# The last inverse-transform stage's table built by masked sines ahead of the work, its factor moved to a neighbouring table, and another order

## The chip, the core and the metric

The kernel runs on one core of a Trainium2 chip. Its time is device time in microseconds (us) of one execution, as a median of several. Engines are named as in the profile: PE (TensorE matmul), PEld (its weight load), DVE (VectorE), ACT (ScalarE), POOL (GpSimd), SP (SyncE, which here only issues DMAs).

## The reference

Two independent sequence mixers over 2048 tokens and 640 channels each; their outputs are set side by side. A is a diagonal complex state space, B is a gated long convolution done by FFT of length 4096.

```python
# A: x [2048, 640]
Lam_bar = exp(dt * Lam);  B_bar = ((Lam_bar - 1) / Lam)[:, None] * Bmat
for t in range(L):
    h = Lam_bar * h + x[t] @ B_bar.T
    hs.append(h)
y_a = 2 * real(hs @ Cmat.T) + x * Dskip
# B: q, k, v [2048, 640]
k_shift = 4-tap causal convolution of k with shift_k
kv  = k_shift * v
y   = irfft(rfft(pad(kv)) * rfft(pad(ssm_k)))[:2048]
y_b = q * (y + kv * ssm_D)
out = concatenate([y_a, y_b], axis=-1)          # bf16
```

## The kernel before

**Part A** works on ten column pairs of states. `up2`, `up1`, `up0a/b/c` (L560 for the input products, L581 for the recurrence steps) build block sums of growing length, `coarse` (`cs_...`, L652 to L666) runs the scan over the 128 blocks, `dn3` to `dn0` (L683, L685) carry the states back down, and `C0` to `C15` (L720) project to the output. `gC` (L550) scales the output matrix. Where the add after a `dn` (`ad...`) is on DVE (L703), DVE adds; where it is on ACT (L701), PE adds instead by one more matmul with the identity (L683) and ACT copies.

**Part B** loads k and v (L775, transposing DMAs), convolves and multiplies them (`cm` L198/L199, `ca` L801, `cx` L802), writes the product to DRAM by rows (`pl`, L808, five planes of 128 channels), reads it back in another layout (`rl`, the relay, L818), and transforms it in two halves of 320 channels. A transform is `s1` (L837 wide form with 16 matmuls, L842 narrow form with 32 smaller ones), evicted by L847; `s2` (L861), evicted by L874; a complex product with the filter's transform (`pp pq py pz`, L885 to L892); then back by `r2` (L906), evicted by L911, and `r1` (L927), whose eviction on DVE (L939) multiplies by q. `h` is the filter (`s1h`, `s2h`), `k` the data; `s1k0_5` is group 5 of half 0. Each of the two filter halves must get `addD` (L770, POOL) before its `s1h`.

The stages' sine tables are made on the chip: an iota and an integer multiply on POOL, then a sine on ACT. They are `F1` (for `s1`), `W` (for `s2`; `w_m` L289, `w_q` L291, `w_s` L296), `IDF` (for `r2`; `i_s` L307) and `G` (for `r1`). `G` is needed last. For it, `tables_G` makes four chunks: `g_m` (L327) and `g_q` (L330) on POOL, `g_s` (L332) on ACT into a scratch piece of buffer `AS`, and then twice `g_k` (L198 on DVE or L199 on ACT), which multiply the chunk by `mk[:, el]`, a column per `el` that is 1/2048 on half of the partitions and 0 on the others. `AS` holds the first transform of half 0 until its product is done, so `tables_G` stands behind `middle(0)`.

All buffers are pieces of one SBUF arena, and dependencies are found from the addresses. The order is not a planner's at run time: the string `ORDER` lists every operation with its engine (T is PE, t is PE with the narrow `s1`, V DVE, A ACT, G POOL, S SP) and its first PSUM bank of eight. Each engine runs its operations in that order. An operation that waits holds up all behind it on its engine. PE's matmuls need a free bank, so a late eviction stops PE.

Of the kernel before, what the change touches and what calls it, by code (L numbers as in the profile page):

```python
# [10 lines left out]
FN = mybir.ActivationFunctionType  # L11
# [7 lines left out]
SC = float(TWO_PI / 2 ** 32 * EPS1)  # L19
# [200 lines left out]
def setup(c):  # L220
# [12 lines left out]
          ins=[I3[:, 0:128]])  # L233
# [26 lines left out]
    P.add("mk2", {V: .12}, lambda e: e.tensor_scalar_mul(out=mk, in0=me, scalar1=1.0 / 2048), outs=[mk], ins=[me])  # L260
# [46 lines left out]
    P.add("i_s", {A: .38}, lambda e: e.activation(out=IDF, in_=qi, func=FN.Sin, bias=npi, scale=SC13), outs=[IDF], ins=[qi, npi])  # L307
    c.p31i, c.mk = p31i, mk


def tables_G(c):
# [10 lines left out]
    for ch in range(4):  # L322
        sn = v("AS", 1024 * ch, 1024)
        ri, bh = ch // 2, ch % 2
        full = v("G", 2048 * ch, 2048)
        qc = full.bitcast(i32)
        P.add("g_m", {G: 1.1}, lambda e, qc=qc, ri=ri, bh=bh: e.iota(  # L327
            qc.rearrange("p (b a) -> p b a", a=32), pattern=[[1, 32], [64, 32]], base=2048 + 2048 * ri + 32 * bh,
            channel_multiplier=0), outs=[full])
        P.add("g_q", {G: 1.9}, lambda e, qc=qc: e.tensor_tensor(out=qc, in0=qc, in1=bc(f41s, [128, 1024]), op=ALU.mult),  # L330
              outs=[full], ins=[full, f41s])
        P.add("g_s", {A: 1.07}, lambda e, qc=qc, sn=sn: e.activation(out=sn, in_=qc, func=FN.Sin, scale=SC), outs=[sn], ins=[full])  # L332
        for el in range(2):
            go = Gt[:, ri, 32 * bh:32 * bh + 32, el, :]
            P.add("g_k", {V: .47, G: 2.9, A: 1.02}, lambda e, go=go, el=el, sn=sn: c.SM[e](go, sn.rearrange("p (b a) -> p b a", a=32), mk[:, el:el + 1]),
                outs=[go], ins=[sn, mk])
# [621 lines left out]
def build(c):  # L958
# [5 lines left out]
    setup(c)  # L964
    params(c)
# [59 lines left out]
    tables_G(c)  # L1025
# [17 lines left out]
def plain_order(P):  # L1043
# [127 lines left out]
```

## Time and profile before

| | us |
|---|---|
| median of 3 runs | 199.77 (199.49 to 200.62) |
| the profiled execution, its own time | 200.44 |
| its span, first to last instruction | 198.7 |
| granted PE clock | 0.999 |

The profile is of one execution. A row of a windows view has a stretch of time, and then how long each engine was busy in it (with its count of instructions); a row of a timeline has start, duration, engine, line and shapes, and in brackets how long the engine had been idle and who ended that; a row of a by-form group has the count, busy us and mean ns of one, and idle time before.

### The profile page before, as it was taken

How to read it: one execution, taken by the hardware profiler on the slowest of the kernel's cores; microseconds unless marked ns; L12 is line 12 of the kernel's file. 1: busy time of each engine (PE TensorE's matmuls, PEld its weight loads, DVE VectorE, ACT ScalarE, POOL GpSimd, SP SyncE). 2: the span in 40 equal slices, each digit the busy share in tenths (PEclk: the TensorE clock that was granted, in tenths of full speed). 3: DMA queues.
4: the chain of work that ended last, by engine and by line, in shares of the span. 5: the costliest groups of instructions: out<-in, count | busy, mean ns of one | idle time of the engine just before them, and what ended most of it. 6: DMA issues, size and time to landing. Idle time of an engine off the chain costs nothing.

```text
span 198.7 us, 7834 instructions
## 1 busy us (share of the span) xinstructions
PE 182.5 (92%) x3493; PEld 121.0 (61%) x3493; DVE 162.3 (82%) x231; ACT 135.1 (68%) x165; POOL 69.1 (35%) x62
## 2 busy tenths in 40 slices
PE   7689999989999997896999799999999999999992
PEld 3344555556565764464566666566777777977761
DVE  3640379779998789999999999899999999958551
ACT  2434499878762859998999798999999940650000
POOL 6759930590000000083200762974600016541200
PEclk9999999999999999999999999999999999999999
DMA  4999999899999999699971796221899524555864
GB/s 93 192 188 155 153 189 133 157 171 188 239 204 225 211 209 120 94 184 148 140 209 49 179 153 136 79 61 38 159 182 178 151 69 132 139 132 125 215 156 142
DMA packets 107739, 30.17 MB, mean 152 GB/s; under 512 B 102586, under 2 KB 107066, under 8 KB 107706
## 3 DMA queue, kind: packets, MB, share of 16 engines
q1 hardware_dynamic: 107418, 29.35, 80.6%
q8 instruction: 27, 0.44, 1.0%
q10 hardware_dynamic: 288, 0.33, 0.6%
q14 instruction: 6, 0.05, 0.1%
HBM read 10.99 MB, written 7.86 MB: 95 GB/s over the span
## 4 chain that ended last, share of the span: by engine, by line
PE 59%; ACT 16%; DVE 9%; SPq 7%; issue 5%; DMA 3%; DVEq 0%; ACTq 0%
PE acc L560 18%; PE acc L720 18%; ACT arena L874 8%; PE acc L906 5%; PE acc L581 4%; SPq L494 3%; PE acc L861 3%; PE acc L927 3%; DMA arena<-in_A_x_dram 3%; SPq L526 3%; DVE arena L847 2%; ACT arena L701 2%; PE acc L685 2%; PE acc L837 2%; ACT arena L554 2%
## 5 line engine op out<-in xcount | busy, mean ns | idle before, releaser
L560 PE MATMUL acc<-arena 128*64 128x512 bf16 x400 | 47.8, 389 | 3.0 <-DMA arena<-in_A_x_dram 2.0
L720 PE MATMUL acc<-arena 128*128 128x320 bf16 x320 | 45.9, 300 | 0.5 <-ACT arena L874 0.4
L560 PEld LDWEIGHTS <-arena 128*64 128x64 bf16 x400 | 24.3, 108 | 22.7 <-issue 4.3
L720 PEld LDWEIGHTS <-arena 128*128 128x128 bf16 x320 | 30.2, 98 | 12.7 <-ACT arena L874 0.6
L874 ACT CAST arena<-acc 128x960 bf16<-128x960 f32 (+1 forms) x40 | 34.9, 916 | 1.3 <-PE acc L861 0.9
L847 ACT CAST arena<-acc 128x1024 bf16<-128x1024 f32 x30 | 29.3, 1028 | 2.9 <-PE acc L842 1.5
L861 PE MATMUL acc<-arena 128*64 128x160 bf16 x512 | 22.9, 235 | 2.0 <-ACT arena L847 0.7
L911 ACT CAST arena<-acc 128x1024 bf16<-128x1024 f32 x16 | 15.9, 1037 | 10.5 <-PE acc L906 10.4
L861 PEld LDWEIGHTS <-arena 128*64 128x64 bf16 x512 | 17.9, 110 | 8.1 <-ACT arena L874 3.0
L722 DVE TENSOR_TENSOR arena<-acc,arena 128x640 bf16<-128x640 f32 x16 | 13.1, 820 | 7.4 <-PE acc L720 7.3
L801 POOL TENSOR_TENSOR arena<-arena 128x2048 bf16<-128x2048 bf16 x1 | 4.1, 4067 | 40.2 <-DVE arena L198 40.2
L712 POOL TENSOR_TENSOR arena<-arena 128x640 bf16<-128x640 bf16 x9 | 12.5, 1398 | 14.8 <-DVE arena L722 8.0
L801 DVE TENSOR_TENSOR arena<-arena 128x2048 bf16<-128x2048 bf16 x14 | 17.1, 1221 | 0.3
L890 POOL TENSOR_TENSOR arena<-arena 128x1280 bf16<-128x1280 bf16 x2 | 5.3, 2668 | 32.8 <-DVE arena L888 20.8
L198 DVE TENSOR_SCALAR arena<-arena 128x2048 bf16<-128x2048 bf16 (+2 forms) x24 | 15.5, 656 | 1.0 <-DMA arena<-in_B_k_dram 0.7
L577 DVE CAST arena<-acc 128x1024 bf16<-128x1024 f32 x5 | 6.0, 1222 | 10.9 <-PE acc L560 10.4
L847 DVE CAST arena<-acc 128x1024 bf16<-128x1024 f32 x10 | 12.0, 1220 | 2.4 <-PE acc L842 1.9
L685 PE MATMUL acc<-arena 128*128 128x512 bf16 (+2 forms) x50 | 13.2, 327 | 0.2 <-ACT arena L874 0.2
L939 DVE TENSOR_TENSOR arena<-acc,arena 128x960 bf16<-128x960 f32 (+1 forms) x12 | 12.2, 1037 | 1.4 <-PE acc L927 1.4
L888 POOL TENSOR_TENSOR arena<-arena 128x1280 bf16<-128x1280 bf16 x4 | 10.6, 2641 | 5.8 <-DVE arena L885 5.8
L885 DVE TENSOR_TENSOR arena<-arena 128x2560 bf16<-128x2560 bf16 x8 | 12.1, 1508 | 0.1
L906 PE MATMUL acc<-arena 64*128 64x128 bf16 x320 | 11.9, 225 | 0.1
(144 smaller groups left out, 294.0 us busy)
## 6 DMA issues: line engine op xcount, KB each, us to landing
out_dram<-arena SPq DMA_DIRECT2D x32, 160.0 KB, 2.7
arena<-in_B_ssm_k_dram SPq DMA_DIRECT2D x8, 320.0 KB, 5.2
kv_rows<-arena SPq DMA_DIRECT2D x5, 512.0 KB, 5.2
arena<-kv_rows SPq DMA_DIRECT2D x16, 160.0 KB, 4.8
arena<-in_A_x_dram SPq DMA_DIRECT2D x16, 160.0 KB, 3.0
arena<-in_B_q_dram SPq DMA_DIRECT2D x8, 320.0 KB, 7.5
arena<-in_A_B_im_dram ACTq DMA_DIRECT2D x1, 160.0 KB, 2.4
arena<-in_A_B_re_dram ACTq DMA_DIRECT2D x1, 160.0 KB, 2.6
```

The lines of the kernel that those rows point to most:

```text
L198: vm = lambda e: lambda out, in_, by: e.tensor_scalar_mul(out=out, in0=in_, scalar1=by)
L560: e.matmul(o[64 * r:64 * r + 64], lhsT=self.BT[j][:, r, d, :], rhs=self.XP[:, d, 2 * q:2 * q + 2], start=(d == 0), stop=(d == 4), skip_gro ...
L685: e.matmul(B[:, o:o + 128 * k], lhsT=c.RR[:, n, j, :], rhs=A[:, j, q:q + k, 0:128], start=not by_pe, stop=True, skip_group_check=True)
L712: P.add(f"xd{i}", {PDVE: dve(640, .52), PPOOL: 1.5}, lambda e: e.tensor_tensor(out=ys, in0=ys, in1=c.DR, op=ALU.mult), outs=[ys], ins=[ys, ...
L720: e.matmul(B[:, 512 * b:512 * b + 320], lhsT=lh[j], rhs=self.CT[:, j, 320 * b:320 * b + 320], start=(j == 0), stop=(j == 9))
L722: P.add(f"ev_C{i}", {PDVE: dve(640)}, lambda e, B: e.tensor_tensor(out=ys.rearrange("p (b n) -> p b n", b=2), in0=B.rearrange("p (b n) -> ...
L801: P.add(f"ca{d}_{j}", tt, lambda e: e.tensor_tensor(out=t1, in0=t1, in1=t2, op=ALU.add), outs=[t1], ins=[t1, t2])
L847: P.add(f"e1{what}{hf}_{u}", {PACT: act(1024), PDVE: dve(1024)}, lambda e, B: c.CP[e](out=out, in_=(B.rearrange("p (l n s k) -> p k s l n" ...
L861: e.matmul(B[64 * s:64 * s + 64, 512 * b + 160 * i:512 * b + 160 * i + 160], lhsT=c.W[:, k, 64 * b:64 * b + 64], rhs=self.AS[hf][:, k, 160 ...
L874: c.CP[e](out=out, in_=b.rearrange("p r (k j n) -> p r k j n", k=n, j=4) if nj > 1 else b.rearrange("p r (k x) -> p r k x", k=n))
L906: e.matmul(B[:, 512 * s + 128 * i:512 * s + 128 * i + 128], lhsT=lh[i][s][r], rhs=rh, start=(r == 0), stop=(r == 1), tile_position=(64 * s ...
L911: P.add(f"er2{hf}_{u}", {PACT: act(1024), PDVE: dve(1024)}, lambda e, B: c.CP[e](out=out, in_=B.rearrange("p (s n b) -> p b s n", s=2, n=4 ...
```

## The change

`tables_G` moves ahead of `params`, so it is the first thing after `setup`. The four `g_s` into scratch and the eight `g_k` go; in their place ACT makes eight sines, two for each chunk, that write `G` directly. The mask is in the sine's scale: `mk` is now `SC` (the factor from integer to angle) on half of the partitions and 0 on the others, one column for each `el`, so the sine's angle is 0 where the table must be 0. The integers of a chunk lie where the next chunk's table will be, those of the last chunk in `Y`. The factor 1/2048 goes into `IDF` by one small multiply on DVE (`i_k`). Every operation gets a new number, and `ORDER` is another list.

```diff
-    P.add("mk2", {V: .12}, lambda e: e.tensor_scalar_mul(out=mk, in0=me, scalar1=1.0 / 2048), outs=[mk], ins=[me])
+    P.add("mk2", {V: .12}, lambda e: e.tensor_scalar_mul(out=mk, in0=me, scalar1=SC), outs=[mk], ins=[me])
...
     P.add("i_s", {A: .38}, lambda e: e.activation(out=IDF, in_=qi, func=FN.Sin, bias=npi, scale=SC13), outs=[IDF], ins=[qi, npi])
+    P.add("i_k", {V: .2}, lambda e: e.tensor_scalar_mul(out=IDF, in0=IDF, scalar1=1.0 / 2048), outs=[IDF], ins=[IDF])
...
     for ch in range(4):
-        sn = v("AS", 1024 * ch, 1024)
         ri, bh = ch // 2, ch % 2
-        full = v("G", 2048 * ch, 2048)
+        full = v("G", 2048 * (ch + 1), 2048) if ch < 3 else v("Y", 0, 2048)
         qc = full.bitcast(i32)
...
-        P.add("g_s", {A: 1.07}, lambda e, qc=qc, sn=sn: e.activation(out=sn, in_=qc, func=FN.Sin, scale=SC), outs=[sn], ins=[full])
         for el in range(2):
             go = Gt[:, ri, 32 * bh:32 * bh + 32, el, :]
-            P.add("g_k", {V: .47, G: 2.9, A: 1.02}, lambda e, go=go, el=el, sn=sn: c.SM[e](go, sn.rearrange("p (b a) -> p b a", a=32), mk[:, el:el + 1]),
-                outs=[go], ins=[sn, mk])
+            P.add("g_s", {A: 1.07}, lambda e, qc=qc, go=go, el=el: e.activation(
+                out=go, in_=qc.rearrange("p (b a) -> p b a", a=32), func=FN.Sin, scale=mk[:, el:el + 1]), outs=[go], ins=[full, mk])
...
     setup(c)
+    tables_G(c)
     params(c)
...
     middle(0)
-    tables_G(c)
     b.load_q(0)
...
-    "122G0 128A0 127A0 8G0 56V0 121S0 0G0 50G0 6T7 82G0 21V0 79G0 116G0 7G0 9V0 41G0 479G0 13G0 93V0 16V0 15V0 19V0 35V0 52V0 14V0 "
+    "140S0 141G0 147A0 75V0 76S0 77S0 8G0 146A0 7G0 9V0 13G0 59G0 0V0 3T1 5T4 21V0 110V0 14V0 18V0 57V0 4T4 15V0 16V0 100G0 19V0 "
```

Lines of the new kernel are one lower from L346 on (L332 is now L334, L847 now L846).

**On ACT**, the stretch of the sines. Before, the four sines (L332) and four of the eight masking multiplies (L199, shape 128x32x32; the other four are on DVE) stand late, among the evictions of the second half's transform and of `r2` (L874, L847, L911). The first piece begins at the first sine:

```order
L332 ACTIVATE arena<-arena 128x1024
L874 CAST arena<-acc 128x2x3x4x40
L332 ACTIVATE arena<-arena 128x1024
L701 CAST arena<-acc 128x8x128
L874 CAST arena<-acc 128x2x3x4x40 x2
L847 CAST arena<-acc 128x64x2x8 x5
L701 CAST arena<-acc 128x8x128
L847 CAST arena<-acc 128x64x2x8 x2
L332 ACTIVATE arena<-arena 128x1024
```

Now (the second piece, from the first eviction of an `up2`, L576) two masked sines (L334) stand near the start, with `sin` of part A (L453), three small exponentials (L368), the first `w_s` (L296), and two multiplies of the convolution (L199) behind them:

```order
L576 CAST arena<-acc 128x2x4x128
L334 ACT_TABLE_LOAD
L334 ACTIVATE arena<-arena 128x32x32 x2
L453 ACTIVATE arena<-arena 128x1280
L368 ACT_TABLE_LOAD
L368 ACTIVATE arena<-arena 128x10 x3
L296 ACT_TABLE_LOAD
L296 ACTIVATE arena<-arena 128x1024
L199 ACTIVATE arena<-arena 128x2048 x2
L394 ACTIVATE arena<-arena 128x80
L576 CAST arena<-acc 128x2x4x128
```

All eight sines and `cos` (L454) now stand ahead of the first eviction of `s2h0`; the table loads are four in all, six before.

**On POOL**, from `addD` of half 0 (L770, now L769) on. Before, one `rr` table (L437), one `g_q` and two `g_m` followed it, then a part of the convolution (L801):

```order
L770 TENSOR_TENSOR arena<-arena 128x80
L437 TENSOR_TENSOR arena<-arena 128x1280
L330 TENSOR_TENSOR arena<-arena 128x1024
L327 IOTA arena 128x1024 x2
L801 TENSOR_TENSOR arena<-arena 128x2048
```

Now three `g_q` (L330) with a `g_m`, then `phc` (L452, which `cos` reads), `r16` (L641, on DVE before) and `gm` (L436, on DVE before) follow it, ahead of the same part of the convolution:

```order
L769 TENSOR_TENSOR arena<-arena 128x80
L330 TENSOR_TENSOR arena<-arena 128x1024
L327 IOTA arena 128x1024
L330 TENSOR_TENSOR arena<-arena 128x1024
L452 TENSOR_TENSOR arena<-arena 128x1280
L641 COPY arena<-arena 128x1280
L330 TENSOR_TENSOR arena<-arena 128x1024
L436 TENSOR_TENSOR arena<-arena 128x1280
L800 TENSOR_TENSOR arena<-arena 128x2048
```

**On SP**, the first loads. Before, behind the first pair of x, both pairs of part A's B matrix (L494) came ahead of the second pair of x (L526) and of the first k (L775):

```order
L526 DMA_TRANSPOSE arena<-in_A_x_dram 128x5x256 x2
L494 DMA_TRANSPOSE arena<-in_A_B_re_dram 128x5x256
L494 DMA_TRANSPOSE arena<-in_A_B_im_dram 128x5x256 x2
L494 DMA_TRANSPOSE arena<-in_A_B_re_dram 128x5x256
L526 DMA_TRANSPOSE arena<-in_A_x_dram 128x5x256 x2
L775 DMA_TRANSPOSE arena<-in_B_k_dram 128x2048
L768 DMA arena<-in_B_ssm_k_dram 32x80x64
L526 DMA_TRANSPOSE arena<-in_A_x_dram 128x5x256 x2
```

Now the second pair of x and the first k stand between the two pairs of B:

```order
L525 DMA_TRANSPOSE arena<-in_A_x_dram 128x5x256 x2
L493 DMA_TRANSPOSE arena<-in_A_B_im_dram 128x5x256
L493 DMA_TRANSPOSE arena<-in_A_B_re_dram 128x5x256
L525 DMA_TRANSPOSE arena<-in_A_x_dram 128x5x256 x2
L774 DMA_TRANSPOSE arena<-in_B_k_dram 128x2048
L493 DMA_TRANSPOSE arena<-in_A_B_im_dram 128x5x256
L493 DMA_TRANSPOSE arena<-in_A_B_re_dram 128x5x256
L525 DMA_TRANSPOSE arena<-in_A_x_dram 128x5x256
```

PE follows: it takes the `up2` of three column pairs with the first B, then the same three with the second pair of x, then those of the second B. Elsewhere the order also moves adds from ACT to DVE (on ACT 11 of 21 before, 6 now), takes the narrow form for 15 of the 40 `s1` groups (25 before), puts three of the sixteen `C` ahead of the second half's `s2k` (four before) and eight between there and the first `r2` of the second half (six before).

72 rows, old and new, of the table ORDER are left out of this document.

## The prediction

> **What bounds the kernel now.** I read the page's busy times first, then a windows view cut where PE starts a new kind of work, then the timeline rows at those cuts, then PE's waits.
>
> ```profile
> PE 182.5 (92%) x3493; PEld 121.0 (61%) x3493; DVE 162.3 (82%) x231; ACT 135.1 (68%) x165; POOL 69.1 (35%) x62
> ```
> ```profile
> core 0: us, PE busy (x) PEld busy (x) DVE busy (x) ACT busy (x) POOL busy (x), PEclk, DMA share, GB/s
> ...
> 20.20:82.70 62.50, 59.47 (x978) 36.44 (x978) 52.50 (x72) 46.56 (x66) 14.13 (x12) 1.00 1.07 180
> 82.70:138.20 55.50, 50.85 (x1210) 33.73 (x1210) 52.92 (x59) 52.38 (x58) 24.70 (x11) 1.00 0.65 121
> 138.20:169.50 31.30, 31.17 (x621) 23.36 (x620) 30.39 (x36) 22.93 (x26) 8.93 (x6) 1.00 0.76 144
> 169.50:195.10 25.60, 25.46 (x588) 19.59 (x584) 17.42 (x19) 5.89 (x6) 6.04 (x5) 1.00 0.66 161
> ```
> ```profile
> 82.73 0.44 PE L842 MATMUL acc<-arena 64*64 64x64 bf16 x32 [0.52 <-ACT arena L874]
> 138.21 1.02 PE L861 MATMUL acc<-arena 128*64 128x160 bf16 x23
> 169.47 1.71 PE L906 MATMUL acc<-arena 64*128 64x128 bf16 x48
> ```
>
> PE's 92% hides stages with different limits. The cuts are the first `s1k0` (82.7), the first `s2k1` (138.2) and the first `r2` of half 1 (169.5). Up to 82.7 PE has gaps. In the **middle** (82.7 to 138.2) PE is busy 50.85 of 55.5, but DVE 52.92 and ACT 52.38: both evicting engines are at 95%, so work on them, not on PE, sets the length. From 138.2 on PE has no gap of note (31.17 of 31.30, 25.46 of 25.60), so PE's work sets it; PE ends at 195.1, and the last stores take 198.7 - 195.1 = 3.6. The start waits for loads:
>
> ```profile
> PE acc L560 <- DMA arena<-in_A_x_dram: 2.0, 2, 1.2
> ```
> ```profile
> 12.36 7.04 PE L560 MATMUL acc<-arena 128*64 128x512 bf16 x60 [0.89 <-DMA arena<-in_A_B_im_dram]
> 20.20 13.82 PE L560 MATMUL acc<-arena 128*64 128x512 bf16 x120 [0.80 <-DMA arena<-in_A_x_dram]
> 14.84 5.23 DMA arena<-in_A_x_dram
> 7.77 3.36 SPq L494 DMA_TRANSPOSE arena<-in_A_B_im_dram  x2
> ```
>
> PE's second group of `up2` waited 0.89 for the first B, the third 0.80 for the second pair of x, whose second transfer (from the chain of waits) started at 14.84 and took 5.23. The last row is SP's: two transposing loads of B hold its queue for 3.36.
>
> This execution took 200.44 us (span 198.7 and 1.74 around it), 0.67 above the median of 199.77. I sum against 200.44 and take 0.67 off at the end. About 0.5%, 1.0 us, is what a measurement of this kernel can tell from no change.
>
> **The tables themselves.**
>
> ```profile
> L332 ACT ACTIVATE arena<-arena 128x1024 bf16<-128x1024 int32 x4 | 4.4, 1112 | 0.0
> L199 ACT ACTIVATE arena<-arena 128x1024 bf16<-128x1024 bf16 x4 | 4.5, 1172 | 0.0
> L198 DVE TENSOR_SCALAR arena<-arena 128x1024 bf16<-128x1024 bf16 x4 | 1.8, 480 | 0.0
> L369 ACT ACT_TABLE_LOAD x2 | 2.6, 1283 | 0.0
> ```
>
> ACT loses 4 x 1.112 + 4 x 1.172 = 9.1 us and gets eight masked sines. No row has one; the nearest is L199, which has the same scale per partition and strided output: 8 x 1.172 = 9.4 (by L332 8.9). DVE loses 4 x 0.480 = 1.9 and gets `i_k`, smaller than L198's rows, at most 0.5. Two of six table loads go, 2 x 1.283 = 2.6. So the totals hardly change; what changes is where the work stands.
>
> ```profile
> 13.18 0.46 ACT L307 ACTIVATE arena<-arena 128x192 bf16<-128x192 int32 x1 [4.68 <-DVE arena L306]
> 13.65 1.28 ACT L369 ACT_TABLE_LOAD   x1
> ```
>
> In these rows a load starts at 13.65, right where the activation before it ends (13.64). [...]
>
> **Up to the first `s1k0`** (82.7 before). Between the same places on PE, sums of rows' means by the two orders give ACT 50.1 to 62.9, less the two loads, so +10.2; DVE 57.0 to 58.9; POOL 22.1 to 33.8; PE 66.7 to 67.9. ACT was busy 46.56 of 62.5 there, so 10 us more fit only if they lie in its gaps. What PE needs at the end of this stretch is the relay:
>
> ```profile
> 68.36 0.57 SPq L808 DMA_DIRECT2D kv_rows<-arena  x1
> 75.69 3.78 SPq L818 DMA_DIRECT2D arena<-kv_rows  x3
> ```
> ```profile
> arena<-kv_rows SPq DMA_DIRECT2D x16, 160.0 KB, 4.8
> ```
>
> The third plane is written at 68.36, after its `cx2` on DVE; the last three reads of half 0 are issued from 75.69, one about 1.26 apart, the last at 78.2, and land 4.8 later, at 83.0: where PE starts (82.73, though by the row its last wait was for an eviction). Now `k2` is loaded ahead of a `C0`, `pl2` has one `C0` less ahead, but four reads come after it besides one `C`, and `coarse` operations stand in DVE's queue before `cx2`. Their sizes are alike, so I leave the relay where it is. For a gain: the second pair of x has two loads of B fewer ahead, so its second transfer starts at 14.84 - 3.36 = 11.5 and lands 5.23 later, at 16.7. PE then has three `up2` with the first B, 2.35 each (7.04 / 3), the second from 12.36, and so wants that x at 12.36 + 2 x 2.35 = 17.1: just in time. That frees the 0.80 before 20.20, and with the other gaps of this stage (62.50 - 59.47 = 3.0) perhaps 2 in all. For a loss: behind its first eviction of an `up2`, near 12.5, ACT has three table loads (3.8), two sines (2.3), `sin`, `w_s`, two multiplies of the convolution and small ones, some 13 in all by their rows. So the next eviction starts near 26, and PE, at 2.35 for each `up2`, needs that bank near 28. If the margin goes, PE waits one to one, some 3 at most. I take **82.9**, bounds 80.7 to 85.7.
>
> **The middle** (55.5 before).
>
> ```profile
> L701 ACT CAST arena<-acc 128x1024 bf16<-128x1024 f32 x9 | 9.2, 1038 | 0.9 <-PE acc L685 0.8
> L703 DVE TENSOR_TENSOR arena<-acc,arena 128x1024 bf16<-128x1024 f32 x8 | 9.7, 1221 | 1.3 <-PE acc L685 1.2
> L847 ACT CAST arena<-acc 128x1024 bf16<-128x1024 f32 x30 | 29.3, 1028 | 2.9 <-PE acc L842 1.5 <-PE acc L837 1.1
> L847 DVE CAST arena<-acc 128x1024 bf16<-128x1024 f32 x10 | 12.0, 1220 | 2.4 <-PE acc L842 1.9 <-PE acc L837 0.5
> L888 DVE TENSOR_TENSOR arena<-arena 128x1280 bf16<-128x1280 bf16 x12 | 9.7, 820 | 0.2
> L801 DVE TENSOR_TENSOR arena<-arena 128x2048 bf16<-128x2048 bf16 x14 | 17.1, 1221 | 0.3
> ```
>
> Between the first `s1k0` and the first `s2k1` ACT loses eight copies of `ad` (8 x 1.038 = 8.3) and three sines (3 x 1.112 = 3.3), and gets two evictions of `s1` (2.1) and two smaller copies (1.4): with small items 57.8 to 49.5. DVE gets four adds (4 x 1.221 = 4.9) and `coarse` work (3.3), and loses two evictions (2.4), one `ca` (1.2), two smaller adds (1.6), five product operations that POOL takes (5 x 0.820 = 4.1), three masking multiplies (1.4), and three evictions of C and gC (2.5): with small items 56.8 to 51.2. PE loses a C (2.8) and most identity matmuls, 46.0 to 39.2, so PE is further from binding.
>
> Before, of 56.8 and 57.8 of work by place 52.92 and 52.38 lay in the time window (0.931, 0.907; the rest ran on either side). The same shares now give 47.7 on DVE and 44.9 on ACT, 92.6 together against 105.3. With the same share of busy time, 55.5 x 92.6 / 105.3 = 48.8; I take **49.0**. Lower bound: DVE without a gap, 47.7. Upper bound: DVE with before's own ratio, 47.7 x 55.5 / 52.92 = 50.0. POOL gets 5 product operations more for this; it was busy 24.70 of 55.5, so it has room.
>
> **From the first `s2k1`** (31.3 and 25.6 before).
>
> ```profile
> L720 PE MATMUL acc<-arena 128*128 128x320 bf16 x320 | 45.9, 300 | 0.5 <-ACT arena L874 0.4
> ```
>
> The cover in PE moved: this stretch gets two C (2 x 45.9 / 16 = 5.7) and four downs that stood in the middle, PE 29.2 to 37.0; DVE 32.4 to 38.5; ACT 25.3 to 21.3. So most of what the middle gains comes back here: PE at 37.0 with 2% of gaps is 37.7, with before's own ratio 37.0 x 31.3 / 29.2 = 39.7. I take **38.4**. DVE, 38.5 x 30.39 / 32.4 = 36.1, stays below. After the first `r2` of half 1 one C goes, PE 25.1 to 22.3: 25.6 - 2.8 = **22.8**. The 3.6 of the tail is the last stores and stays.
>
> **Sum:** 82.9 + 49.0 + 38.4 + 22.8 = 193.1; with 3.6 of tail and 1.74 around it 198.4, against 200.44: 2.0 less. On the median, 199.77 - 2.0 = **197.8**. Gains: 6.5 in the middle and 2.8 at the end; losses 7.1 between. It is a difference of larger terms, and that sets the range: the bounds give 80.7 + 47.7 + 37.7 + 22.7 = 188.8 to 85.7 + 50.0 + 39.7 + 22.9 = 198.3, thus 193.5 to 203.0 (with 3.6 + 1.74 - 0.67 = 4.67).
>
> **Rivals.**
>
> *All gains, no loss at the start* (0.13). The early loads and the shorter C chain bring the relay forward to 80.7, and both PE stretches run gapless: 188.8 + 4.67 = 193.5. For it: PE has 3.0 of gaps between 20.2 and 82.7. Against it: the relay's write follows DVE's chain, and DVE gets 1.9 more.
>
> *No change* (0.23). ACT's and DVE's queues in the middle wait for each other as before and the next stretch keeps its ratio: 83.0 + 50.0 + 39.7 + 22.8 + 4.67 = 200.2. For it: the same PE work, only redistributed, and PE is 92% busy. Against it: the middle is the one stage where PE has 4.65 of gaps, and the work of both binding engines falls by 12%.
>
> *Slower by POOL's queue* (0.20).
>
> ```profile
> 36.90 0.68 POOL L770 TENSOR_TENSOR arena<-arena 128x80 bf16<-128x80 bf16 x1 [10.44 <-DMA arena<-in_B_ssm_k_dram]
> L330 POOL TENSOR_TENSOR arena<-arena 128x1024 int32<-128x1024 int32 x4 | 7.6, 1892 | 0.0
> L327 POOL IOTA arena<- 128x1024 int32 x4 | 4.3, 1079 | 0.0
> L453 POOL TENSOR_TENSOR arena<-arena 128x1280 int32<-128x1280 int32 x1 | 2.3, 2318 | 0.0
> L437 POOL TENSOR_TENSOR arena<-arena 128x1280 bf16<-128x1280 bf16 x1 | 3.6, 3580 | 0.0
> L454 ACT ACTIVATE arena<-arena 128x1280 bf16<-128x1280 int32 x1 | 1.3, 1280 | 0.0
> ```
> ```profile
> 5.88 1.89 POOL L291 TENSOR_TENSOR arena<-arena 128x1024 int32<-128x1024 int32 x1 [1.77 <-DVE arena L303]
> 6.41 1.39 DVE L410 TENSOR_TENSOR arena<-arena 128x10 f32<-128x10 f32 x1
> 7.72 0.15 DVE L409 TENSOR_TENSOR arena<-arena 128x10 f32<-128x10 f32 x1
> ```
>
> `addD` waits for its load until 36.9 and ends at 37.6. Behind it now stand a `g_q`, a `g_m`, a `g_q`, `phc`, `r16` and a `g_q`: 1.89 + 1.08 + 1.89 + 2.32 + about 2.8 (a copy has no POOL row; it lies between L327's 1.08, which reads nothing, and L437's 3.58, which reads two; I stay nearer to the latter) + 1.89 = 11.9, so 49.5 if nothing holds them. But something does: the tiny add L410, alone 0.15 like its neighbour L409, took 1.39 and ended only as POOL's multiply (5.88 + 1.89 = 7.77) did; the two don't run together. [...] DVE's convolution adds in that time (`ca`, `cx`, some six of 1.22) come to 7.3, so POOL's last `g_q` may end at 56.8 and the last sines and `cos`, 1.28 + 3 x 1.17 on ACT, at about 61.6. They stand ahead of the eviction of `up0a_0`, which PE wants near 60 to 61. From there each further us of POOL delay is one of PE; from about 3 late the change is slower than before (the 2.0 gained, and 1.0): with POOL held for two more instructions, 2 x 1.8, it is 197.8 + 3.6 = 201.4. For it: all eight sines must be done before `s2h0`'s first eviction. Against it: POOL was busy 14.13 of 62.5 in this stage, so it has time, and DVE need not stand against each of its instructions.
>
> **How the numbers follow.** Forecast 0.44 (its own range 196.3 to 198.7), rivals 0.13, 0.23, 0.20. Range 193.8 to 202.0: below it lies a good half of the first rival (0.08), above it half of the slower case (0.10), whose delay can go on to the 203.0 of the bounds. Faster by over 0.5% is 0.44 + 0.13 = 0.57, within it 0.23, slower 0.20.
>
> **What would show it.** The gap of PE at 20.20 gone; L334 with eight rows of about 1.17; four table loads. First `s1k0` between 80.7 and 85.7, with the third plane written near 68. The stretch to the first `s2k1` 48 to 50, DVE and ACT at 93 to 96% in it; the next 37.7 to 39.7 with PE over 97%; the last 22.8. If ACT, before the eviction of `up0a_0`, waits for POOL, the slower rival is right. The forecast is wrong if PE's gaps in the middle do not shrink, or if the work taken out of it returns as more than the 7.1 priced in.

## The result, and the profile after

| | before | changed | ratio, 95% interval |
|---|---|---|---|
| median of 20 runs, us | 200.25 (199.49 to 201.75) | 198.59 (195.50 to 201.15) | 0.992 (medians) |
| comparison as measured | | | 0.985 (0.981 to 0.988) |
| mean granted PE clock | 0.999 (traced) | 0.989 to 0.991 in 10 of the 20, 0.997 to 1.000 in the others | |

The changed kernel is faster, by 0.8% on the medians and by 1.5% in the comparison, which leaves out executions over 1.5% above the fastest of their kernel, here 13 of the 20 with all ten at a lowered clock among them. The medians are therefore the fairer figure, because in this kernel the lowered clock follows a stop of its own PE (2.06 us in the trace, with 1.7 us of missing clock behind it), as the runs below show. Its times spread over 5.7 us, those of before over 2.3. The ten at the lower clock have a median of 200.0, which is no gain over before, the other ten 198.2. The kernel before isn't free of the lowered clock: of the 61 executions of it beside the experiments, 13 have a mean of 0.980 to 0.991.

The windows view of the changed kernel, cut at the same places on PE as before (columns: stretch, length, then PE, PEld, DVE, ACT and POOL busy, granted clock, DMA share, GB/s):

```profile
20.20:81.09 60.89, 58.77 (x924) 37.08 (x918) 51.40 (x65) 51.70 (x68) 16.99 (x11) 1.00 1.16 182
81.09:134.12 53.03, 45.64 (x1063) 31.96 (x1061) 48.17 (x49) 46.39 (x53) 22.72 (x10) 0.97 0.79 134
134.12:172.96 38.84, 38.56 (x670) 27.86 (x670) 36.69 (x44) 19.59 (x23) 14.45 (x6) 1.00 0.53 120
172.96:195.70 22.74, 22.71 (x564) 17.84 (x564) 16.91 (x20) 6.62 (x7) 2.75 (x2) 1.00 0.71 173
```

Early stage 81.1 (82.7 before), middle 53.0 (55.5), then 38.8 (31.3) and 22.7 (25.6). The middle has a granted clock of 0.97. The same view in steps of 1 us shows where:

```profile
102.00:103.00 1.00, 0.00 (x0) 0.00 (x0) 0.90 (x2) 0.25 (x1) 1.00 (x1) 1.00 1.19 344
103.00:104.00 1.00, 0.76 (x17) 0.61 (x18) 1.00 (x3) 0.03 (x1) 0.50 (x1) 0.84 1.05 353
104.00:105.00 1.00, 1.00 (x6) 0.17 (x6) 0.64 (x2) 0.98 (x1) 0.00 (x0) 0.50 0.81 296
105.00:106.00 1.00, 1.00 (x20) 1.00 (x20) 1.00 (x1) 0.11 (x1) 0.00 (x0) 0.50 0.52 83
106.00:107.00 1.00, 1.00 (x24) 1.00 (x22) 0.42 (x2) 0.84 (x1) 0.00 (x0) 0.50 0.62 107
107.00:108.00 1.00, 1.00 (x40) 1.00 (x36) 1.00 (x2) 0.56 (x1) 0.00 (x0) 0.95 0.01 1
```

PE stands still, and then runs at half its clock. The missing clock adds up to 0.16 + 3 x 0.50 + 0.05 = 1.7 us, which at a clock of 0.50 is 3.4 us of time. The timeline rows around it, of SP, POOL, DVE and PE (start, duration, engine, line; in brackets the wait ahead):

```profile
86.24 7.85 SPq L767 DMA_DIRECT2D arena<-in_B_ssm_k_dram  x4
94.13 2.37 SPq L710 DMA_DIRECT2D arena<-in_A_x_dram  x1
...
99.29 2.61 POOL L887 TENSOR_TENSOR arena<-arena 128x1280 bf16<-128x1280 bf16 x1
99.72 2.53 DVE L711 TENSOR_TENSOR arena<-arena 128x640 bf16<-128x640 bf16 x1 [0.63 <-DMA arena<-in_A_x_dram]
102.36 0.82 DVE L721 TENSOR_TENSOR arena<-acc,arena 128x640 bf16<-128x640 f32 x1
103.24 0.70 PE L836 MATMUL acc<-arena 128*64 128x128 bf16 x16 [2.06 <-DVE arena L721]
```

From the top: four loads of the second filter half hold SP for 7.85 us; the x load of `C0` is issued only after them; DVE's `xd0` (L711) waits 0.63 for it and, once begun, needs 2.53 us, until POOL's product L887 has ended (99.29 + 2.61 = 101.9); so the add of `C0` (L721) frees its PSUM bank late, and PE's next group wanted that bank.

The tables did what the diff says: eight sines, and four table loads.

```profile
L334 ACT ACTIVATE arena<-arena 128x1024 bf16<-128x1024 int32 x8 | 8.8, 1140 | 0.1
```

### The profile page after: what moved, and what is told of

Its sections match the earlier page's. It is cut to its first block, busy times and chain, and to the rows that moved or that the text cites. A ratio compares the mean times of both kernels' runs of the same rounds, so it can differ in the third digit from the quotient of the medians.

```text
span 199.3 us, 7475 instructions
## 1 busy us (share of the span) xinstructions
PE 181.9 (91%) x3324; PEld 123.4 (62%) x3324; DVE 163.0 (82%) x225; ACT 135.8 (68%) x166; POOL 73.1 (37%) x62
## 4 chain that ended last, share of the span: by engine, by line
PE 52%; DMA 14%; DVE 11%; ACT 11%; SPq 7%; issue 3%; ACTq 0%; DVEq 0%
PE acc L559 18%; PE acc L719 16%; ACT arena L873 6%; DMA arena<-in_A_x_dram 5%; PE acc L860 4%; PE acc L905 4%; SPq L767 4%; DMA arena<-in_B_k_dram 3%; DMA kv_rows<-arena 2%; ACT arena L846 2%; DMA arena<-in_A_B_re_dram 2%; PE acc L684 2%; PE acc L580 2%; DVE arena L721 2%; PE acc L926 2%
## 5 line engine op out<-in xcount | busy, mean ns | idle before, releaser
L873 ACT CAST arena<-acc 128x960 bf16<-128x960 f32 (+1 forms) x41 | 36.2, 916 | 9.2 <-PE acc L860 7.3
L559 PEld LDWEIGHTS <-arena 128*64 128x64 bf16 x400 | 24.4, 108 | 21.2 <-issue 2.6
L846 ACT CAST arena<-acc 128x1024 bf16<-128x1024 f32 x29 | 27.7, 1054 | 3.0 <-PE acc L836 2.3
L910 ACT CAST arena<-acc 128x1024 bf16<-128x1024 f32 x17 | 16.2, 1035 | 16.4 <-PE acc L905 16.4
L860 PE MATMUL acc<-arena 128*64 128x160 bf16 x512 | 23.7, 238 | 1.4 <-ACT arena L873 0.8
L887 POOL TENSOR_TENSOR arena<-arena 128x1280 bf16<-128x1280 bf16 x6 | 16.7, 2790 | 20.7 <-DVE arena L884 20.7
L860 PEld LDWEIGHTS <-arena 128*64 128x64 bf16 x512 | 18.3, 111 | 9.2 <-ACT arena L873 3.6
L702 DVE TENSOR_TENSOR arena<-acc,arena 128x1024 bf16<-128x1024 f32 (+1 forms) x15 | 17.2, 1166 | 2.4 <-PE acc L684 2.0
L836 PE MATMUL acc<-arena 128*64 128x128 bf16 x400 | 15.2, 227 | 4.3 <-DVE arena L721 2.1
L721 DVE TENSOR_TENSOR arena<-acc,arena 128x640 bf16<-128x640 f32 x16 | 13.2, 823 | 6.8 <-PE acc L719 5.7
L836 PEld LDWEIGHTS <-arena 128*64 128x64 bf16 x400 | 12.9, 115 | 6.6 <-DVE arena L721 2.2
L846 DVE CAST arena<-acc 128x1024 bf16<-128x1024 f32 x11 | 13.1, 1219 | 4.5 <-PE acc L836 3.9
L889 POOL TENSOR_TENSOR arena<-arena 128x1280 bf16<-128x1280 bf16 x3 | 7.8, 2609 | 19.6 <-DVE arena L887 19.5
L684 PE MATMUL acc<-arena 128*128 128x512 bf16 (+2 forms) x50 | 12.4, 337 | 0.8 <-ACT arena L873 0.7
L199 ACT ACTIVATE arena<-arena 128x2048 bf16<-128x2048 bf16 (+2 forms) x10 | 11.0, 1110 | 2.7 <-DMA arena<-in_B_k_dram 2.7
L711 POOL TENSOR_TENSOR arena<-arena 128x640 bf16<-128x640 bf16 x4 | 5.8, 1458 | 17.5 <-DMA arena<-in_A_x_dram 17.5
L576 DVE CAST arena<-acc 128x1024 bf16<-128x1024 f32 x4 | 4.9, 1225 | 8.8 <-PE acc L559 8.8
```

What stands on the lines that cost most here:

```text
L559: e.matmul(o[64 * r:64 * r + 64], lhsT=self.BT[j][:, r, d, :], rhs=self.XP[:, d, 2 * q:2 * q + 2], start=(d == 0), stop=(d == 4), skip_gro ...
L684: e.matmul(B[:, o:o + 128 * k], lhsT=c.RR[:, n, j, :], rhs=A[:, j, q:q + k, 0:128], start=not by_pe, stop=True, skip_group_check=True)
L702: e.tensor_tensor(out=o, in0=b, in1=o, op=ALU.add)
L721: P.add(f"ev_C{i}", {PDVE: dve(640)}, lambda e, B: e.tensor_tensor(out=ys.rearrange("p (b n) -> p b n", b=2), in0=B.rearrange("p (b n) -> ...
L836: e.matmul(B[64 * b:64 * b + 64, 128 * i:128 * i + 128], lhsT=lh[i], rhs=F[:, b, :], start=True, stop=True, tile_position=(0, 64 * b))
L846: P.add(f"e1{what}{hf}_{u}", {PACT: act(1024), PDVE: dve(1024)}, lambda e, B: c.CP[e](out=out, in_=(B.rearrange("p (l n s k) -> p k s l n" ...
```

## The experiments

The question was first whether the stop of PE and the half clock belong together and what makes the stop, then what the terms of the forecast are worth. All kernels ran in five rounds beside the kernel before. Where a kernel is set against another of a different chip, the ratios to before are compared, not the times.

**1. The changed kernel again.**

> The changed kernel as it is, for a second trace. In its first trace PE stood still from 101.2 to 103.2 us (waiting for the DVE add L721 behind the multiply L711) and its granted clock was 0.50 from about 104 to 107. Theory 'stall and clock': that stall varies from execution to execution, and those whose mean granted clock is 1.00 lack the stall or have a shorter one; a trace at clock 1.00 has a span near 194 to 197, a middle (first s1k0 to first s2k1) of 49 to 51 instead of 53.0, and PE's longest wait there under 1 us. Rival 'clock by itself': the clock falls without PE having stood still, and a trace at 1.00 shows the same 2.06 us wait.

Measured: 199.57 (196.39 to 199.68), before 200.35 on this chip. Five of six executions have a clock of 0.991, at 198.95 to 199.68; the one at 1.00 took 196.39. The traced one was again of the five, with the same wait:

```profile
PE acc L836 <- DVE arena L721: 2.1, 1, 2.1
```

So there is no trace at clock 1.00, and this run decides nothing by itself. It shows that the stop is no accident of one execution, and the missing clock behind it is again 1.7 us. Its early stage ended at 79.6, its middle took 52.6.

**2. The x load ahead of the filter loads.** In the order, 693 is that load, 420 to 423 the filter's:

```diff
-422S0 420S0 421S0 ... 423S0 ... 415A0 693S0 408T4
+693S0 422S0 420S0 421S0 ... 423S0 ... 415A0 408T4
```

> One DMA moved on SP: the first natural-layout load of x (L710) goes ahead of the four loads of the second filter half (L767), which held SP for 7.9 us. Theory 'stall and clock': L711 then runs before POOL's L887 starts and takes 0.48 instead of 2.53 us, PE's wait of 2.06 us goes, no execution shows a clock of 0.99, and the time is 195 to 196.5 in nearly all executions (2 to 3.5 us under the median of the changed kernel). Rival 'clock by itself': the wait goes, but the clock still falls in about half of the executions; gain at most 2. Rival 'the filter loads are late instead': s1h1 waits for the filter half that now comes 0.4 to 2 us later, and the time stays within 0.5 us.

Measured: 196.64 (196.10 to 197.97), ratio 0.981 (0.977 to 0.986); every execution at a clock of 0.996 or more. DVE's `xd0` started before POOL's product:

```profile
98.43 0.48 DVE L711 TENSOR_TENSOR arena<-arena 128x640 bf16<-128x640 bf16 x1
```

and the windows view of the middle reads

```profile
80.52:129.98 49.46, 44.16 (x1064) 31.00 (x1062) 45.85 (x49) 46.11 (x53) 22.34 (x10) 1.00 0.82 144
```

49.5 where the changed kernel has 53.0: 3.6 less, of 2.06 + 1.7 = 3.8 that the stop and the half clock amount to. One moved DMA gains 2.9 us on the median of the same chip, as expected, though the times lie just above the expected 195 to 196.5. "Stall and clock" stands. "Clock by itself" falls: the stop is also gone in experiments 9, 10 and 12, and all 24 executions of these four have 0.996 or more, where 15 of the 26 of the changed kernel have 0.991 or less.

**3. More matmuls in the wait.**

```diff
-            for i in range(8):
+            for i in [i for _ in range(5 if (what, hf, u) == ("h", 1, 5) else 1) for i in range(8)]:
```

> The 32 matmuls of s1h1_5, which stand just ahead of PE's wait of 2.06 us, are issued five times (the same result), some 1.8 us more of PE work inside the wait; nothing else changes. Theory 'stall and clock': the clock stays at 1.00 in all executions although DVE is as late as before; executions that had the stall gain 1.5 to 2 us, executions without it lose 1 to 1.8, and the spread of the times halves. Rival 'clock by itself': the clock falls in as many executions as before and the time is the same or longer.

Measured: 199.33 (198.00 to 201.77); ten of eleven executions at 0.997 or more, one at 0.991. The clock held nearly as expected. The time did not fall and its spread did not halve (3.8 us, 3.3 in the first run); whether the extra matmuls cost what the clock gave back is not shown. The traced execution is no test of the wait, since there `xd0` began just before POOL's product:

```profile
97.98 0.68 DVE L711 TENSOR_TENSOR arena<-arena 128x640 bf16<-128x640 bf16 x1
98.26 2.87 POOL L887 TENSOR_TENSOR arena<-arena 128x1280 bf16<-128x1280 bf16 x1
```

The trace also has a new wait of PE of 1.68 us at 103.2 for "issue", for which no view gives a cause.

**4. The sines twice.**

```diff
-                out=go, in_=qc.rearrange("p (b a) -> p b a", a=32), func=FN.Sin, scale=mk[:, el:el + 1]), outs=[go], ins=[full, mk])
+                out=go, in_=qc.rearrange("p (b a) -> p b a", a=32), func=FN.Sin, scale=mk[:, el:el + 1]) for _ in range(2)], outs=[go], ins=[full, mk])
```

> Each of the eight masked sines is made twice in place, 9.1 us more ACT work before the first s1k0. The prediction held that the sines moved there lie in ACT's gaps with a margin of some 1.4 us and then cost PE one to one. By that the time grows by 4 to 8 us (9.1 less the margins left in ACT's 60.9 us stage, of which 51.7 are busy). Rival 'the place is free': it grows by less than 2, so ACT's early stage had much more room.

Measured: 205.27 (203.89 to 207.49), 5.7 more than the first run. Part of that is clock, since two of the six executions have 0.981 and 0.983; the four at 0.989 to 0.992 have a median of 204.6, 5.0 above the five of the first run at 0.991. So 9.1 us of ACT work cost about 5, and the place has room for some 4 us beyond the eight sines that are there. The margin of 1.4 that the expectation names stands nowhere in the prediction, which has about 2 (26 against 28). PE waits for an eviction behind the sines:

```profile
PE acc L580 <- ACT arena L625: 3.0, 1, 3.0
```

**5. Two relay reads back behind the third plane.** 391 is the write of the plane, 396 and 393 are reads. This and the next three are edits of the kernel of experiment 2.

```diff
-394S0 ... 396S0 ... 393S0 ... 391S0 ... 392S0
+394S0 ... 391S0 396S0 393S0 ... 392S0
```

> Against the kernel of the second experiment (one x load ahead of the filter loads, 196.6 us). Two of the relay's reads of half 0, which the change put ahead of the write of the third plane (pl2), go back behind it, so that seven reads follow pl2 as before the change, not five. Theory 'the relay sets the end of the early stage': the last read is issued 2 x 1.26 = 2.5 us later, the first s1k0 groups wait for kv_rows, s1k0 begins or stalls 1.5 to 2.5 us later, and the time grows by 1 to 2.5. Rival 'PE's own work sets it' (PE is busy 58.8 of 60.3 us there): the time stays within 0.7.

Measured: 197.62 (196.57 to 198.50), ratio 0.986 against 0.981, intervals that overlap. The trace is clearer than the time:

```profile
PE acc L836 <- DMA arena<-kv_rows: 1.8, 1, 1.8
```

PE waits 1.8 us for the relay, `s1k0` starts at 82.2 instead of 80.5, the middle then takes 49.3, as without the edit (49.5). The relay sets the end of the early stage when seven reads follow the plane.

**6. Two operations from POOL back to DVE.**

```diff
-296G0 ... 156G0
+296V0 ... 156V0
```

> Against the kernel of the second experiment (196.6 us). r16 (L641) and gm (L436) go back from POOL to DVE. Theory 'DVE has room for neither': 0.8 and 1.5 us more stand in DVE's queue ahead of cx2 and so ahead of pl2 and the relay; the time grows by 0.5 to 2. Rival of the prediction, 'POOL's queue is what holds the sines': POOL's last g_q ends near 46 instead of 57.9, and the time falls by 0.5 or more. Third reading, 'neither binds' (PE's work does): within 0.5.

Measured: 197.65 (197.17 to 197.84), ratio 0.986 (0.983 to 0.989) against 0.981. POOL's last `g_q` ends at 47.0 in its trace, 11.5 us earlier than in the changed kernel, and the last sines still start only at 55.95 (57.70 there), behind the evictions ahead of them on ACT. It is not faster: POOL's queue does not hold the sines. It is slower by 0.4% on ratios whose intervals meet; so "DVE has room for neither" and "neither binds" are not told apart (the trace shows no new long wait before `s1k0`, which starts at 80.2).

**7. Four adds back to ACT.**

```diff
-330V2 ... 338V4 ... 332V2 ... 336V0
+330A2 ... 338A4 ... 332A2 ... 336A0
```

> Against the kernel of the second experiment (196.6 us). The four adds ad1_0, ad1_2, ad1_6 and ad1_8 go back from DVE to ACT, as before the change: ACT gets four copies (4 x 1.04 = 4.2 us), DVE loses four adds (4 x 1.22 = 4.9), PE gets eight identity matmuls (8 x 0.22 = 1.8). Theory 'DVE and ACT bind the middle together' (45.9 and 46.1 of 49.5 us busy): ACT now has 50.3 us of work in the middle, which becomes 51 to 53, and the time grows by 1.5 to 3.5. Rival 'DVE alone binds': the middle shrinks, the time falls by 0.5 to 3. Rival 'waits between engines set it, not either's sum': within 0.7.

Measured: 200.63 (199.76 to 202.18), ratio 1.001 (0.999 to 1.004): these four adds are worth 4.0 us by the ratios, 0.5 over the expected range. The middle is 52.4, 3.0 longer, as expected:

```profile
80.83:133.27 52.44, 45.56 (x1070) 31.60 (x1069) 41.74 (x45) 49.63 (x57) 23.31 (x10) 1.00 0.80 135
```

ACT is now busy 49.63 of it and DVE 41.74; together that is 91.4, hardly other than the 92.0 of experiment 2. So the length follows the busier of the two engines (95% here, 93% there), not their sum. PE's wide `s1` groups (L836) wait 1.8 us there for ACT's evictions of `s1`, against 0.7. In the traced execution PE also waits 1.55 for "issue" at 188.1.

**8. The early loads as before.**

```diff
-164S0 163S0 153S0 152S0 161S0 162S0 359S0 155S0 154S0
+164S0 163S0 153S0 152S0 155S0 154S0 161S0 162S0 359S0
```

> Against the kernel of the second experiment (196.6 us). The second pair of B's loads goes ahead of the second pair of x again, as before the change; PE's order stays. Theory: the second pair of x lands 3.4 us later, near 20, PE waits for it 2.5 to 3.3 us where it now runs without a gap from 12.6 to 35.6, and of that 0.8 to 3.3 reach the end. Rival 'the early stage's end hangs on the relay or on ACT, not on PE's start': the wait is there, and the time grows by less than 0.7.

Measured: 200.38 (198.83 to 201.25), ratio 0.998 (0.996 to 1.001): 3.4 us by the ratios. PE waits for x as expected:

```profile
PE acc L559 <- DMA arena<-in_A_x_dram: 3.2, 2, 2.7
```

In the trace, at a clock of 1.00, the first `s1k0` comes 1.9 us later (82.38), so most of the wait reaches it. The lower clock can account for the rest: eight of the twelve executions have 0.988 to 0.991, and the four others a median of 199.4. This prices the loads within the new order on PE, which wants x early; before the change PE used the second B first and lost only 0.8.

**9. `xd0` on POOL**, in the changed kernel:

```diff
-424G0 ... 694V0
+694G0 424G0
```

> Against the changed kernel itself (199.6 us; its x load still behind the filter loads, landing near 99.0 us). The multiply xd0 (L711) goes from DVE to POOL, ahead of addD1 and the product L887, so that no POOL instruction with SBUF inputs stands against it. Theory 'the late load makes the wait only because POOL's L887 starts in the same 0.3 us and shuts DVE's L711 out (2.53 us in place of 0.48)': xd0 takes some 1.5 us on POOL, the add L721 starts within 0.5 us of C0's end, PE's wait of 2.06 us becomes 0 to 0.8, no half clock follows, and the time is 196 to 198. Rival 'the load alone makes it late': the wait stays over 1.5 us and the time stays at 199 to 200.

Measured: 197.01 (195.93 to 197.95), ratio 0.980 (0.976 to 0.984), all clocks 0.997 or more, and no such stop of PE (between 94 and 106 us its longest wait is 0.28). In the traced execution x landed before 97.3, early enough for either engine, so it doesn't tell the late load from POOL's product.

**10. A multiply on ACT behind the sine that follows it.**

```diff
-373A0 ... 70A0 129A0
+70A0 129A0 373A0
```

> Against the kernel of the second experiment (196.6 us). On ACT the multiply cm1_2, which waits 1.9 to 2.7 us for the landing of k1, goes behind the masked sine and the small multiply that follow it, so that these 1.35 us lie in its wait. Theory: the evictions behind it come up to 1.35 us earlier, PE's waits for L600 near 50 us (0.6 in that trace, 1.2 in the first trace of the changed kernel, 0 in the second) go, first up0a at 50.2 instead of 51.3, and the time falls by 0.3 to 1.2 with less spread. Rival 'the relay sets the end of the stage': PE only waits longer for kv_rows, the time stays within 0.3.

Measured: 196.33 (195.85 to 197.49), ratio 0.976 (0.972 to 0.980) against 0.981 of experiment 2. `up0a` starts at 50.5 instead of 51.3 and PE's wait for L600 near 50 us (0.6 in experiment 2) is gone; the stage ends at 79.8 instead of 80.5. A gain of some 0.5% by the ratios, on intervals that overlap. It is the fastest version tried.

**11. The narrow form as before** in 14 groups:

```diff
-184T2 172T0 188T4 186T2 404T2 414T0 408T4 501T0 503T0 509T4 511T6 499T6 497T2 597T0
+184t2 172t0 188t4 186t2 404t2 414t0 408t4 501t0 503t0 509t4 511t6 499t6 497t2 597t0
```

> Against the kernel of the second experiment (196.6 us). The 14 s1 groups that the change turned from the narrow to the wide form are narrow again: 14 x (0.54 - 0.36) = 2.6 us less PE work, 14 x 16 more matmuls and as many weight loads to fetch. Prediction's view 'PE's work in s1 is not what binds': the time stays within 0.7, because nearly all of these groups lie where ACT and DVE evict. Rival 'PE binds up to the first s1k0': the four groups there give 0.7, and the time falls by 0.7 to 2.6. Rival 'more instructions cost fetches': PE waits for issue over 1 us somewhere, and the time grows by 1 or more.

Measured: 198.02 on the median, ratio 0.984 (0.980 to 0.988). Its trace is of an execution at a clock of 0.76 (228 us), so its waits can't be set beside the others. By the other times (197.13 to 198.38) it isn't faster: 2.6 us less PE work, by the expectation's sum, buys nothing, so PE's work in `s1` does not bind. Why it is rather slower (0.3% on overlapping intervals) stays open; waits for "issue", the third reading, are not excluded.

**12. POOL's product behind `xd2`**, in the changed kernel; 704 is `xd2`, 455 the product:

```diff
-455G0 ... 704G0
+704G0 455G0
```

> Against the changed kernel itself (199.6 us), loads as there. On POOL the multiply xd2 (L711, which waits for its own later x load) goes ahead of the product L887, so that nothing of POOL with SBUF inputs starts in the 0.6 us in which DVE's xd0 waits for its x. The ninth run did not separate the two causes, because there x landed 2 us earlier than in the first trace. Theory 'the shut-out on POOL makes the wait': xd0 still starts 0 to 0.8 us after the product L884, but takes 0.48 instead of 2.5 us; PE's wait of 2.06 becomes 0 to 0.7; no half clock in any execution; 196 to 198 us. Rival 'the late load alone': PE's wait stays over 1.5 us and most executions stay at a mean clock of 0.991 and 199 to 200 us.

Measured: 196.84 (195.80 to 197.77), ratio 0.982 (0.977 to 0.986), all clocks 0.997 or more. The x load is late again, and the multiply takes 0.49:

```profile
98.74 0.49 DVE L711 TENSOR_TENSOR arena<-arena 128x640 bf16<-128x640 bf16 x1 [0.52 <-DMA arena<-in_A_x_dram]
99.22 1.40 POOL L711 TENSOR_TENSOR arena<-arena 128x640 bf16<-128x640 bf16 x1 [0.59 <-DVE arena L711]
100.58 2.62 POOL L887 TENSOR_TENSOR arena<-arena 128x1280 bf16<-128x1280 bf16 x1
```

The first row waits 0.52 for x, nearly the 0.63 in the changed kernel; no POOL instruction stands against it, and PE's wait is gone (0.28 is its longest between 94 and 106 us, where the changed kernel has 2.06). The shut-out by POOL's product (2.53 in place of 0.49) makes the wait; the late load only brings the two instructions together.

## Why the prediction was right, and where its steps were not

The forecast was 197.8, 1.0% under before; the medians say 0.8%, the comparison 1.5%. That the number came so near is in part luck. By the trace the four stretches sum to 195.7 where 193.1 was forecast: 1.8 less early, 4.0 more in the middle, 0.3 more behind it. The traced execution is one of the ten at the lower clock and lies 2.5 above the median; the median is near the forecast because the other ten lack the half clock.

**The early stage, 82.9 forecast, 81.1 and 79.6 in two traces.** The step that failed is "Their sizes are alike, so I leave the relay where it is". The order puts two more reads ahead of the third plane, so only five follow it (the prediction counts four), where seven did. The SP rows of the changed kernel show the last one issued by 76.7 (before 79.5), though the plane is written later (69.5 against 68.4):

```profile
69.51 0.34 SPq L807 DMA_DIRECT2D kv_rows<-arena  x1
69.90 0.42 SPq L817 DMA_DIRECT2D arena<-kv_rows  x1
70.37 1.92 SPq L534 DMA_TRANSPOSE arena<-in_A_C_re_dram  x1
72.70 3.95 SPq L817 DMA_DIRECT2D arena<-kv_rows  x4
```

Experiment 5 prices that at 1.7 us of `s1k0`. So the relay would have set the end with seven reads behind the plane, and with five it no longer does: the first `s1k0` follows PE's own matmuls without a wait.

```profile
80.94 0.22 PE L684 MATMUL acc<-arena 128*128 128x128 bf16 x1
81.09 0.64 PE L836 MATMUL acc<-arena 128*64 128x128 bf16 x16
```

The relay is close behind: in the second trace the next group waits 0.67 for it. PE's gap at 20.2 went as forecast, and experiment 8 shows that it hangs on the loads.

**The middle, 49.0 forecast, 53.0 and 52.6.** Without the stop it is 49.5 (experiment 2) and 49.6 (experiment 12: `s1k0` at 80.22, `s2k1` at 129.78). So without the stop the size was right, and that the evicting engines set it stands: DVE is busy 45.85 and ACT 46.11 of the 49.46, 92.0 together where 92.6 was forecast. The rule behind the size, one length for the sum of both engines, does not stand: in experiment 7 the sum is 91.4 and the middle 52.4. The size came out because the two are nearly equal both before (52.92 and 52.38) and after. What the forecast lacked is one wait of 2.06 us and 1.7 us of missing clock after it. The prediction had a row of the mechanism, DVE's L410 at 1.39 in place of 0.15 beside a POOL multiply, but looked for it only at POOL's work on the sine tables. The x loads of the `C` on SP were not followed at all.

**The rest, 38.4 and 22.8 forecast, 38.8 and 22.7.** Right: PE's work sets it, and the cover that moved there comes back as time. PE is busy 38.56 there, 1.6 more than the 37.0 that the rows gave, and has less in gaps than was added for them.

**Its own signs.** The prediction names two signs that it is wrong, and both came. PE's gaps in the middle did not shrink: 4.65 before, 7.4 now (53.03 - 45.64), and 5.3 without the stop. PE's work fell by 5.2 there, so a shorter middle need not have smaller gaps, and the sign was badly chosen. And the work returned as 7.5 (38.84 - 31.30), a little more than the 7.1 priced in.

**The rivals.** *POOL's queue* fell, though POOL's last `g_q` ended even later than its 56.8, at 58.5.

```profile
55.38 1.25 POOL L641 COPY arena<-arena 128x1280 f32<-128x1280 f32 x1 [10.75 <-PE acc L836]
56.59 1.90 POOL L330 TENSOR_TENSOR arena<-arena 128x1024 int32<-128x1024 int32 x1
57.70 3.42 ACT L334 ACTIVATE arena<-arena 128x1024 bf16<-128x1024 int32 x3
61.48 1.64 ACT L625 CAST arena<-acc 128x512 bf16<-128x512 f32 x4 [0.36 <-PE acc L580]
```

What held it there was not DVE: `r16` (L641) overwrites filter data that PE still reads, and waited 10.75 for it (it took 1.25, where 2.8 was taken). The 7.3 us that DVE's adds put on POOL in the 56.8 no run shows: ahead of that wait POOL's L330 took 1.89 and 1.90 and L452 2.32, as before the change, and it was DVE's add L801 that took 3.24 beside L452, in place of 1.23. On ACT the last sines run without a gap, and the evictions behind them (L625) wait for PE, so nobody waits for POOL, and experiment 6 gains nothing by unloading it. *No change* fell on the median, since the middle did shrink, but its 200.2 is what the ten executions at the lower clock have. *All gains* (193.5) was not reached: the fastest execution of the changed kernel took 195.5.

**The sines' price** (8 x 1.17 forecast) was 8 x 1.140, and experiment 4 shows that their place has room for some 4 us more.

## What to carry to other kernels

When an order moves DMAs past each other, count for each awaited transfer how many issues stand ahead of it in its queue, before and after (two reads more behind the plane moved `s1k0` by 1.7 us in experiment 5); and follow the small late loads of side work too: here a multiply that waited 0.63 us for one, and then ran beside POOL's product, held a PSUM bank for which PE waited 2.06. When times scatter, look at the granted clock beside them: the stop of 2.06 us was followed by 1.7 us of missing clock. Where one DVE instruction stretches beside one of POOL, as `xd0` did (2.53 us), try another order: the one moved DMA of experiment 2 brought it to 0.48 and the one moved instruction of experiment 12 to 0.49.

## What was not expected of the hardware

*A stop of 2.06 us was followed by half the clock, one of 2.97 was not.* The stop of 2.06 us (2.15 in the second trace) was followed by some 3.4 us at 0.50. In the trace of experiment 4 a longer one was not: PE waited 2.97 us up to 67.12 (a timeline row) and the clock stayed at 1.00 (the third number from the end of the rows by 1 us),

```profile
67.12 0.97 PE L580 MATMUL acc<-arena 128*64 128x128 bf16 x28 [2.97 <-ACT arena L625]
```
```profile
66.00:67.00 1.00, 0.00 (x0) 0.00 (x0) 0.04 (x1) 1.00 (x3) 0.00 (x0) 1.00 0.92 78
...
68.00:69.00 1.00, 1.00 (x38) 1.00 (x34) 0.00 (x0) 0.95 (x4) 0.00 (x0) 1.00 0.00 0
```

while 0.50 came later in the same trace (from 110 us on) after the stop of 2.1 us at `xd0`. In experiment 8, a stop of 2.7 us left the traced clock at 1.00, but eight of its twelve executions have 0.988 to 0.991. Where the lowered clock of the other kernels begins (13 of 61 executions of before, one each of experiments 5 and 11) no trace shows. What besides a stop decides whether the clock falls is not shown: in the traces the longer stops (2.97 and 2.7) left it at 1.00, and of the changed kernel, with a lowered mean in 15 of 26 executions, no trace shows whether the other 11 have the stop.

*Tenths of a us decided who shut out whom.* `xd0` took 2.53 where it began 0.43 behind POOL's product (changed kernel), and 0.68 where it began 0.28 ahead of it (experiment 3). Both directions show in the rows: the multiply took 2.53 in place of 0.48 behind the product, and the product 2.87 in place of 2.61 behind the multiply.
